# Decode attention with a gated FFN: one loop turn per head group on all engines, V in one load

## The chip, the core and the metric

The kernel runs on one core of one Trainium2 chip. The core has five engines that run their own instruction streams: TensorE (PE in the profile; its weight loads are PEld), VectorE (DVE), ScalarE (ACT), GpSimd (POOL) and SyncE (SP), which issues the transfers. They meet only at semaphores: an instruction may wait until a semaphore has reached a value, and may raise one when it is done. Data come from HBM over 16 DMA engines into SBUF (128 partitions); TensorE writes its results into PSUM. The metric is the device time of one execution in microseconds (us). Before the change it is 354.29 us, the median of three runs (353.94 to 354.31).

## The reference

One token passes through two branches, and a scalar gate mixes them. Branch A is attention over a cache: 32 query heads in 8 groups of 4, each group with its own K and V of 32768 rows of 128 numbers. Branch B is a SwiGLU feed-forward layer with 1792 hidden units.

```python
def _A_ref(x, k_cache, v_cache, wq, wo):          # x: (1, 1, 512)
    q = (x @ wq).reshape(B, Sq, 32, 128).transpose(0, 2, 1, 3)
    k = jnp.repeat(k_cache, 4, axis=1)             # k_cache: (1, 8, 32768, 128)
    v = jnp.repeat(v_cache, 4, axis=1)
    scores = jnp.einsum("bhqd,bhkd->bhqk", q, k) * (128 ** -0.5)
    p = softmax(scores, axis=-1)
    o = jnp.einsum("bhqk,bhkd->bhqd", p, v)
    return o.transpose(0, 2, 1, 3).reshape(B, Sq, 4096) @ wo

def _B_ref(x, w_gate, w_up, w_down):
    return (silu(x @ w_gate) * (x @ w_up)) @ w_down

x = A_x
g = sigmoid((x * gate_w).sum(-1, keepdims=True))
return g * _A_ref(x, ...) + (1 - g) * _B_ref(x, ...)
```

All arrays are bf16. K and V are 64 MiB each; with the weights the kernel reads 148.1 MB.

## The kernel before

**Pages.** SBUF holds five pages of 4 MiB (`page`, 128 partitions of 32 KiB). A page takes half of one group's K or V: block `b` (0 or 1) of 16384 rows, partition `p` holding 128 rows that follow each other. Pages 0 and 2 are for K, 1 and 3 for V; page 4 holds `wq` at first and `wo` at the end, and page 3 holds `w_gate` and `w_up` before V comes into it.

**Queue.** SP issues all transfers, in one order written out by hand: `wq`, `x`, `gate_w`, `w_gate`, `w_up`, then K and V pages, then `w_down` (`wd`) and `wo` in five pieces. From group 2 on, K block `b` of group `g` alternates with V block `b` of group `g-1`. A K page waits on `sem_fill` until its page has been transposed for the group before, a V page on `sem_v_free` until the matmuls on it are through. The very last V block goes into page 0, which K has left.

**Start.** `x` and `gate_w` are loaded as columns, 4 numbers per partition. POOL builds two identities, a permutation `pmat` and a selection `sel4` by `affine_select`, and sums the gate's product over the partitions (L263). PE makes q (L440, L457) and the hidden units of branch B (L470, L482), ACT the sigmoids, VectorE the rest.

**K block (`emit_k`).** A block has 8 units of 8 transposes. A unit transposes 16 rows of every partition (as fp32 pairs, L340) into one of two PSUM buffers `pst`; VectorE copies it to SBUF (`ktT`, L669); 16 matmuls of 8 columns make the scores (L352) in `ps_sc[b]`. PE runs two units ahead of the copies. VectorE then takes each partition's maximum (L674), for both blocks together L676.

**Softmax.** POOL takes the maximum over all partitions with `partition_all_reduce` (L268). ACT scales it to `nbias` (L553) and takes eight exponentials per group (L562, four heads by two blocks) that also sum.

**V block (`emit_v`).** 32 matmuls with 512 columns, in four strips of PE's columns (L399), add into `ps_o`. After both blocks ACT copies `ps_o` to `acc` (L574), PE reduces the strips by matmuls with `sel4` (`emit_reduce`, L378), and VectorE copies the result into `oT` (L660).

**Order of groups.** On PE the groups run in a hardware loop of 8 turns; a turn handles K block `b` of group `g`, then V block `b` of group `g-1`, for `b` = 0 and 1. Group 7's V comes in the end section. ACT, VectorE and POOL have their eight groups written out one after another. The exponentials of group `g` and the accumulator copy of group `g-1` so run on ACT while PE is at other work.

**End (`emit_end`).** V of group 7, the sum of exponentials for all 32 heads in one fp32 matmul (L501), the reciprocals, branch B's `wd` (L411, 14 matmuls), a scaled and transposed attention output (`oTs`, `O2a`, `O2`), and `wo` in strips of one row (L411) and, for its last eight pieces, in rows (L422). The end section stands in the code ahead of the start section; a loop of two turns and two branches select them.

Of the kernel before, what the change touches and what calls it, by code (L numbers as in the profile page):

```python
# [5 lines left out]
ACT = mybir.ActivationFunctionType  # L6
ALU = mybir.AluOpType
# [3 lines left out]
ReduceOp = bass.bass_isa.ReduceOp  # L11


def bass_gated_mix__gqa_block_cached__swiglu_ffn__decode_kernel(
# [27 lines left out]
    BLK = 128 * R  # L42
    NB = S // BLK
    assert S % BLK == 0 and NB == 2
# [22 lines left out]
    QT = H * DH // (NSTRIP * QN)  # L67
    assert QT == 2 and QN == 512 and F % (NSTRIP * FC) == 0 and FS <= 512
    assert RQ * HPG <= 32 and RQ * DH == 512

    PG_K = (0, 2)
    PG_V = (1, 3)
# [4 lines left out]
    with ExitStack() as es:  # L77
# [3 lines left out]
        sem_page = [S_(f"s_page{i}") for i in range(4)]  # L81
        sem_vl = S_("s_vl")
# [5 lines left out]
        sem_ld_wd = S_("s_ld_wd")  # L88
        sem_fill = S_("s_fill")
        sem_sc = S_("s_sc")  # L90
        sem_v_free = S_("s_v_free")
        sem_cp = S_("s_cp")
        sem_out = S_("s_out")
        sem_const = S_("s_const")
        sem_pool = S_("s_pool")
        sem_ident = S_("s_ident")
        sem_dchain = S_("s_dchain")
        sem_pz = S_("s_pz")
        sem_pe_t = S_("s_pe_t")
        sem_pe_part = S_("s_pe_part")  # L100
        sem_part = S_("s_part")
        sem_ps1 = S_("s_ps1")
        sem_pe_q = S_("s_pe_q")
        sem_pe_qp = S_("s_pe_qp")
        sem_pe_h = S_("s_pe_h")
        sem_pe_S = S_("s_pe_S")
        sem_pe_O2 = S_("s_pe_O2")
        sem_pe_sum = S_("s_pe_sum")
        sem_dve_prod = S_("s_dve_prod")
        sem_dve_gpart = S_("s_dve_gpart")  # L110
        sem_dve_qT = S_("s_dve_qT")
        sem_dve_t1 = S_("s_dve_t1")
        sem_dve_tr = S_("s_dve_tr")
        sem_dve_tm = S_("s_dve_tm")
        sem_dve_tT = S_("s_dve_tT")
        sem_pmax = S_("s_pmax")
        sem_dve_esum2 = S_("s_dve_esum2")
        sem_dve_oT1 = S_("s_dve_oT1")
        sem_dve_oT2 = S_("s_dve_oT2")
        sem_dve_O2 = S_("s_dve_O2")  # L120
        sem_dve_row = S_("s_dve_row")
        sem_act_g = S_("s_act_g")
        sem_act_sg = S_("s_act_sg")
        sem_nbias = S_("s_nbias")
        sem_ps0 = S_("s_ps0")
        sem_acc = S_("s_acc")
        sem_red = S_("s_red")
# [606 lines left out]
```

## Time and profile before

| what | value |
|---|---|
| median of three runs | 354.29 us |
| the profiled execution's own time | 354.33 us |
| its span, first to last instruction | 352.5 us |
| mean granted TensorE clock | 0.827 |
| PE matmul busy | 265.0 us (75%) |
| PE weight loads busy | 223.2 us (63%) |
| VectorE busy | 181.7 us (52%) |
| ScalarE busy | 33.1 us (9%) |
| GpSimd busy | 6.3 us (2%) |
| read from HBM | 148.11 MB, 420 GB/s over the span |
| instructions recorded | 8346 |

The page divides the span into 40 slices of 8.8 us and gives each engine's busy share in tenths. A matmul's record shows an operation in a pipeline, so a busy PE isn't a PE at its peak: eight transposes are 0.93 us apart from the next unit's scores although each record is longer. PE has a granted clock that changes between 0.50 and 1.00 within the run. In the timeline a line gives start, duration, engine, source line, operation, output and inputs, count, and in brackets the idle time before it and what ended that. In the list of waits a line gives the total wait in us, how often, and the longest. DMA work is best read from when its data land: the wait of the first instruction that reads them.

### The profile page before, as it was taken

The page shows a single profiled execution, that of the slowest core. Times are in us where ns is not written, and L with a number is a line of the kernel's source. Part 1 is how long each engine was busy: PE and PEld are TensorE (multiplying, and loading weights), DVE is VectorE, ACT ScalarE, POOL GpSimd, SP SyncE. Part 2 cuts the span into 40 slices and gives each one's busy share as a digit, 9 for nine tenths or more (in the row PEclk, how much of TensorE's full clock was granted, in tenths as well). Part 3 has the DMA queues.
Part 4 walks back from the last instruction along what each step waited for, and adds up shares of the span by engine and source line. Part 5 has one row for each costly group of instructions (what it writes and reads, how often), then busy time and mean ns, then how long its engine had stood idle before and what let it go on. Part 6 is the DMA issues. An engine that isn't in the chain of part 4 may idle for free.

```text
span 352.5 us, 8346 instructions
## 1 busy us (share of the span) xinstructions
PE 265.0 (75%) x3831; PEld 223.2 (63%) x3831; DVE 181.7 (52%) x192; ACT 33.1 (9%) x149; POOL 6.3 (2%) x26
## 2 busy tenths in 40 slices
PE   0343987997999969597797949694987959795385
PEld 0113986976887949395786839493967859493131
DVE  2044967653874938266563818283644838093000
ACT  1000000400040040002100040004000030004000
POOL 0200000000000000000000000000000000000000
PEclk9986989785998998969887978799885989599555
DMA  8999999999999999999999999999999999999993
GB/s 322 409 439 429 433 433 426 431 425 439 435 428 431 431 432 428 439 431 428 428 439 431 428 428 439 435 428 428 439 431 428 428 442 428 428 428 442 407 422 145
DMA packets 6208, 148.22 MB, mean 420 GB/s; under 512 B 952, under 2 KB 952, under 8 KB 1336
## 3 DMA queue, kind: packets, MB, share of 16 engines
q1 hardware_dynamic: 6200, 148.12, 98.1%
q8 instruction: 5, 0.08, 0.1%
q14 instruction: 3, 0.02, 0.0%
HBM read 148.11 MB, written 0.00 MB: 420 GB/s over the span
## 4 chain that ended last, share of the span: by engine, by line
DMA 65%; PE 30%; DVE 3%; SPq 1%; issue 1%
DMA page<-in_A_k_cache_dram 53%; PE pst L340 23%; DMA page<-in_A_wo_dram 12%; PE ps_sc L352 5%; DVE ktT L669 2%; PE ps_o L399 2%; PE pst L422 0%; PE ps_m L378 0%; SPq L304 0%; SPq L326 0%; SPq L275 0%; SPq L319 0%; SPq L300 0%; SPq L297 0%; SPq L296 0%
## 5 line engine op out<-in xcount | busy, mean ns | idle before, releaser
L669 DVE COPY ktT<-pst 128x2048 bf16<-128x2048 bf16 x128 | 156.0, 1224 | 108.5 <-PE pst L340 101.6
L340 PE MATMUL pst<-ident_f,page 128*128 128x128 f32 x1024 | 159.5, 314 | 40.9 <-DMA page<-in_A_k_cache_dram 39.4
L340 PEld LDWEIGHTS pst<-ident_f,page 128*128 128x128 f32 x1024 | 136.0, 163 | 51.5 <-DMA page<-in_A_k_cache_dram 46.9
L352 PE MATMUL ps_sc<-qcur,ktT 128*128 128x8 bf16 x2048 | 68.0, 166 | 8.6 <-DVE ktT L669 8.6
L352 PEld LDWEIGHTS ps_sc<-qcur,ktT 128*128 128x128 bf16 x2048 | 67.2, 97 | 11.4 <-DVE ktT L669 10.0
L399 PE MATMUL ps_o<-page,ET 128*16 128x512 bf16 x512 | 40.0, 468 | 6.4 <-DMA page<-in_A_v_cache_dram 6.4
L399 PEld LDWEIGHTS ps_o<-page,ET 128*16 128x16 bf16 x512 | 12.9, 101 | 22.9 <-issue 8.4
L553 ACT ACTIVATE nbias<-gmax 128x4 f32<-128x4 f32 x8 | 1.6, 205 | 267.0 <-POOL gmax L268 267.0
L562 ACT ACTIVATE ET<-ps_sc,nbias 128x128 bf16<-128x128 f32 x64 | 23.9, 555 | 0.6
L562 ACT ACTIVATION_READ_ACCUMULATOR ET<-ps_sc,nbias 128x1 f32 x64 | 18.2, 284 | 0.0
L674 DVE TENSOR_REDUCE pmaxf<-ps_sc 128x4 f32<-128x512 f32 x16 | 11.1, 692 | 10.4 <-PE ps_sc L352 10.4
L440 PE MATMUL pst<-page,xT 128*1 128x512 bf16 x32 | 3.6, 627 | 14.9 <-DMA xT<-in_A_x_dram 14.9
L378 PE MATMUL ps_m<-sel,acc 128*128 128x4 f32 x72 | 10.9, 275 | 4.1 <-ACT acc L574 4.1
L378 PEld LDWEIGHTS ps_m<-sel,acc 128*128 128x128 f32 x72 | 10.2, 220 | 5.5 <-ACT acc L574 5.5
L440 PEld LDWEIGHTS pst<-page,xT 128*1 128x1 bf16 x32 | 1.0, 115 | 16.6 <-issue 16.6
L268 POOL PARTITION_ALL_REDUCE gmax<-pmax x8 | 3.0, 374 | 291.8 <-DVE pmax L676 291.8
L660 DVE COPY oT<-ps_m 128x4 f32<-128x4 f32 x8 | 1.3, 157 | 13.2 <-PE ps_m L378 13.2
L574 ACT ACTIVATE acc<-ps_o 128x512 f32<-128x512 f32 x8 | 5.2, 652 | 14.8 <-PE ps_o L399 14.8
L603 DVE TENSOR_TENSOR prod_col<-xT,gwT 128x4 f32<-128x4 bf16 x1 | 0.2, 164 | 11.2 <-DMA gwT<-in_gate_w_dram 11.2
L470 PE MATMUL pst<-page,xT 128*1 128x448 bf16 x32 | 3.0, 553 | 1.7 <-DMA page<-in_B_w_up_dram 1.7
L411 PE MATMUL pst<-page,O 128*1 128x512 bf16 x24 | 2.9, 617 | 1.7 <-DMA page<-in_A_wo_dram 1.7
L482 PE MATMUL ps_m<-ones_bf,ktT 128*128 128x1 bf16 x14 | 1.0, 200 | 4.2 <-DVE ktT L649 4.2
(58 smaller groups left out, 31.9 us busy)
## 6 DMA issues: line engine op xcount, KB each, us to landing
page<-in_A_k_cache_dram SPq DMA_DIRECT2D x16, 4096.0 KB, 27.2
page<-in_A_v_cache_dram SPq DMA_DIRECT2D x16, 4096.0 KB, 31.7
page<-in_A_wq_dram SPq DMA_DIRECT2D x1, 4096.0 KB, 13.9
page<-in_A_wo_dram SPq DMA_DIRECT2D x1, 2048.0 KB, 39.6
page<-in_B_w_gate_dram SPq DMA_DIRECT2D x1, 1792.0 KB, 16.9
page<-in_B_w_up_dram SPq DMA_DIRECT2D x1, 1792.0 KB, 20.6
wd<-in_B_w_down_dram SPq DMA_DIRECT2D x1, 1792.0 KB, 35.1
page<-in_A_wo_dram SPq DMA_DIRECT2D x1, 1024.0 KB, 41.6
```

Of the source, the lines that this page charges most:

```text
L268: pool.partition_all_reduce(gmax[:, g, :], pmax[:, g, :], 128, ReduceOp.max).then_inc(sem_gmax, 1)
L340: ins = pe.transpose(pst[u % NST][:, k * 128 : (k + 1) * 128], kv[:, n * 128 : (n + 1) * 128], ident_f[:, :],)
L352: ins = pe.matmul(ps_sc[b][:, col : col + 2 * HPG], kt[:, k, e, :], qcur[:, e, :], start=(e == 0), stop=(e == 1),)
L378: ins = pe.matmul(ps_m[:, M_P0 : M_P0 + HPG], acc[:, q, :], sel4[:, q * HPG : (q + 1) * HPG], start=(q == 0), stop=(q == RQ - 1),)
L399: ins = pe.matmul(ps_o[32 * c : 32 * c + RQ * HPG, :], ET[:, n : n + RQ, :].rearrange("p n h -> p (n h)"), view[:, k * RQ : (k + 1) * RQ, ...
L411: return pe.matmul(ps_c[32 * c : 32 * c + 1, :], vec[:, j : j + 1], w[:, j, :], start=start, stop=stop, skip_group_check=True,)
L440: ins = pe.matmul(pst[0][32 * k : 32 * k + 1, t * QN : (t + 1) * QN], xT[:, c : c + 1], wq_v[:, c, n : n + QN], start=(c == 0), stop=(c == ...
L470: ins = pe.matmul(pst[1][32 * k : 32 * k + 1, w * 512 : w * 512 + FS], xT[:, c : c + 1], wgu[:, w, c, k * FS : (k + 1) * FS], start=(c == ...
L562: act.activation(ET[:, b * R : (b + 1) * R, h], sc[:, h, :], ACT.Exp, bias=nbias[:, g, h : h + 1], scale=SCALE, accum_out=esum[:, g, b, h ...
L574: act.activation(acc[:, :, :].rearrange("p q d -> p (q d)"), ps_o[:, :], ACT.Copy).then_inc(sem_acc, STEP)
L669: dve.tensor_copy(ktT[:, u % NKT, :], pst[u % NST][:, :].bitcast(BF16)).then_inc(sem_cp, 1)
L674: dve.tensor_reduce(pmaxf[:, f, :], sc, AX.X, ALU.max).then_inc(sem_pmax, 1)
```

## The change

All engines now run one hardware loop over the groups, and a turn does one group whole: K block 0, K block 1, the maximum, the exponentials, V, the accumulator copy, the reduction, the reciprocals. Semaphores rise by 16 a turn, so that each wait is the loop's register plus a constant.

- **Loads.** V of a group comes in one transfer of 8 MiB, 64 KiB for each partition, behind both K pages; for the last group in two. K is read as 32 KiB from every 64 KiB, so that a partition has the same 256 rows for K and V. Pages 0 and 1 are for K, 2 and 3 for V. The first V waits for the hidden units of branch B, which lie in page 3. POOL raises the second V semaphore for the groups with one load.
- **Maximum.** The POOL reduction becomes a PE transpose of the 128x4 maxima, a VectorE reduction to four numbers, their product with a 4x4 identity, and a PE matmul with ones that spreads them over the partitions. ACT reads the result from PSUM.
- **Sums.** The sum of exponentials becomes a matmul in every group, with reciprocal and gate on VectorE.
- **Start.** `x` and `gate_w` come as rows of one partition. PE turns `x` into columns (four matmuls) and makes the identity's argument: the row of 0 to 127 against its negative, by two matmuls with ones; VectorE compares with 0 and derives `ident`, `pmat` and `sel4`. The gate's sum is a VectorE reduction along the row and a matmul that spreads it. POOL has only two memsets, and neither library instruction is left.
- **End.** `emit_end` starts with branch B; V and reductions are all in the loop.

Core of the diff:

```diff
-    PG_K = (0, 2)
-    PG_V = (1, 3)
+    PG_K = (0, 1)
+    PG_V = 2
...
+                for g in range(G - 1):
+                    pool.wait_ge(sem_v[0], 16 * (g + 1))
+                    pool.sem_inc(sem_v[1], 16)
...
-                def load_v(g, b):
...
+                    src = A_k_cache[0, g, :, :].rearrange("(p b r) d -> p b r d", b=NB, r=R)
...
+                def load_v(g):
+                    if g:
+                        sp.wait_ge(sem_v_free, STEP * g)
+                    else:
                         sp.wait_ge(sem_pe_h, 1)
...
+                    if g < G - 1:
+                        sp.dma_start(
+                            vpage.rearrange("p b r d -> p (b r d)"),
+                            src.rearrange("p b r d -> p (b r d)"),
+                        ).then_inc(sem_v[0], 16)
...
+                sp.dma_start(x_row[0:1, :], A_x[0, :, :]).then_inc(sem_ld_x, 16)
+                sp.dma_start(gw_row[0:1, :], gate_w.unsqueeze(0)).then_inc(sem_ld_g, 16)
...
-                for b in range(NB):
-                    load_k(0, b)
-                load_v(0, 0)
-                load_k(1, 0)
-                load_v(0, 1)
-                load_k(1, 1)
-                for g in range(2, G):
+                for g in range(G):
                     for b in range(NB):
                         load_k(g, b)
-                        load_v(g - 1, b)
-                for b in range(NB):
-                    load_v(G - 1, b)
+                    load_v(g)
...
+                def emit_max(i):
+                    pe.wait_ge(sem_pm, i + STEP)
+                    pe.transpose(
+                        ps_m[0:HPG, M_A0 : M_A0 + 128], pmax[:, :], ident_f[:, :]
+                    ).then_inc(sem_t, STEP)
+                    pe.wait_ge(sem_dg, i + STEP)
+                    pe.matmul(
+                        ps_m[:, M_B0 : M_B0 + HPG],
+                        ones_f[0:HPG, :],
+                        diag[:, :],
+                        start=True,
+                        stop=True,
+                    ).then_inc(sem_b, STEP)
...
                 def emit_reduce(i):
-                    pe.wait_ge(sem_acc, i)
-                    pe.wait_ge(sem_rc, i)
+                    pe.wait_ge(sem_es, i + STEP)
+                    pe.matmul(
+                        ps_s,
+                        ones_f[:, :],
+                        esum2[:, :],
+                        start=True,
+                        stop=True,
+                    ).then_inc(sem_s, STEP)
+                    pe.wait_ge(sem_acc, i + STEP)
...
                     with pe.Fori(0, G * STEP, STEP) as i:
                         for b in range(NB):
                             emit_k(i, b)
-                            with pe.If(i > 0):
-                                emit_v(i, b)
+                        emit_max(i)
+                        emit_v(i)
+                        emit_reduce(i)
...
+                with act.Fori(0, G * STEP, STEP) as i:
+                    act.wait_ge(sem_b, i + STEP)
                     act.activation(
-                        nbias[:, g, :], gmax[:, g, :], ACT.Copy, scale=-SCALE
-                    ).then_inc(sem_nbias, 1)
...
+                        nbias[:, :], ps_m[:, M_B0 : M_B0 + HPG], ACT.Copy, scale=-SCALE
+                    ).then_inc(sem_nbias, STEP)
+                    act.wait_ge(sem_nbias, i + STEP)
...
+                    act.wait_ge(sem_v_free, i + STEP)
+                    act.activation(part, ps_o[:, :], ACT.Copy).then_inc(sem_acc, STEP)
...
+                with dve.Fori(0, G * STEP, STEP) as i:
                     for b in range(NB):
                         for u in range(UPP):
-                            dve.wait_ge(sem_fill, UPP * f + u + 1)
+                            dve.wait_ge(sem_fill, i + (UPP * b + u + 1))
...
+                    dve.wait_ge(sem_t, i + STEP)
+                    dve.tensor_reduce(
+                        gm[:, :], ps_m[0:HPG, M_A0 : M_A0 + 128], AX.X, ALU.max
+                    ).then_inc(sem_d, 1)
+                    dve.wait_ge(sem_d, i + 3)
+                    dve.tensor_scalar(
+                        diag[:, :], ident_f[0:HPG, 0:HPG], gm[:, 0:1], None, op0=ALU.mult
+                    ).then_inc(sem_dg, STEP)
+                    dve.wait_ge(sem_exp, i + STEP)
+                    dve.tensor_tensor(
+                        esum2[:, :], esum[:, 0, :], esum[:, 1, :], ALU.add
+                    ).then_inc(sem_es, STEP)
+                    dve.wait_ge(sem_s, i + STEP)
+                    dve.reciprocal(rS[:, :], ps_s).then_inc(sem_d, 1)
...
+                    dve.wait_ge(sem_red, i + STEP)
```

The semaphore on the exponentials that PE held ahead of a block's scores is gone, since V of the group stands between.

482 lines of the change are left out of this document (216 added, 266 removed).

## The prediction

> **What bounds the kernel now.** I read the page's slices and its chain first, then the waits, then the timeline of single groups.
>
> ```profile
> DMA  8999999999999999999999999999999999999993
> GB/s 322 409 439 429 433 433 426 431 425 439 435 428 431 431 432 428 439 431 428 428 439 431 428 428 439 435 428 428 439 431 428 428 442 428 428 428 442 407 422 145
> ...
> DMA 65%; PE 30%; DVE 3%; SPq 1%; issue 1%
> ```
>
> The queues are full from the first slice to the last. 148.1 MB at about 429 GB/s is 345 us of the 352.5 us span, so the kernel is bound by its bytes. The waits say how much room TensorE has:
>
> ```profile
> PE pst L340 <- DMA page<-in_A_k_cache_dram: 39.4, 13, 4.7
> PE ps_o L399 <- DMA page<-in_A_v_cache_dram: 6.4, 2, 6.1
> PE pst L440 <- DMA xT<-in_A_x_dram: 14.9, 1, 14.9
> ```
>
> TensorE waits 39.4 us for K and 6.4 us for V over eight groups, some 5.7 us a group. The last wait falls before the loop. So all that the change puts in line on TensorE must fit in those 5.7 us, or the bound moves.
>
> The rate of the loads: the first K page lands at 33.0, the last one, 28 pages later, at 306.36. That is 273.4/28 = 9.76 us for a 4 MiB page and **39.05 us for a group** of four pages.
>
> **What a group costs on TensorE.** In the timeline a K block (8 units of 8 transposes, VectorE copy, 16 score matmuls) comes in two prices, by the clock in which it begins:
>
> ```profile
> 81.95 5.38 PE L340 MATMUL pst<-ident_f,page 128*128 128x128 f32 x24 [2.32 <-DMA page<-in_A_k_cache_dram]
> ...
> 95.72 1.90 PE L399 MATMUL ps_o<-page,ET 128*16 128x512 bf16 x32
> 97.55 1.97 PE L340 MATMUL pst<-ident_f,page 128*128 128x128 f32 x16
> ...
> 109.35 1.03 PE L378 MATMUL ps_m<-sel,acc 128*128 128x4 f32 x8
> ```
>
> The block from 81.95 to 95.72 took 13.8 us: it followed a wait, and the granted clock was 0.50 for its first five microseconds. The one from 97.55 to 109.35 took 11.8 us at clock 1.00. Thirteen blocks after a wait lie between 12.7 and 13.8, about 13.2 on the mean. The clock falls when there is little work in a stretch of about 3.4 us (it changed at 36.4, 46.6, 50.0, 60.3, 67.1) and rises after a full stretch of work.
>
> **The change, part by part.** First the order of work. Before, K of one group stood beside V of the previous one, so maximum, exponentials and accumulator copy lay under matmuls. After, every engine does group g whole: K, K, maximum, exponentials, V, copy, reduction. What was hidden stands in line now. My sum for one group on TensorE:
>
> 1. First K block: 13.2 (it begins after a thin stretch, so at the low clock).
> 2. Second K block: 12.4. It follows the first with no gap. Group 0, the only such pair in the trace, took 13.2 for it, since the clock fell after the thin tail of the first block; the best block took 11.8. I take the middle.
> 3. From the last score to the first V matmul: 5.75, worked out here from these rows:
>
> ```profile
> 59.03 0.56 PE L352 MATMUL ps_sc<-qcur,ktT 128*128 128x8 bf16 x16 [0.54 <-DVE ktT L669]
> 59.63 0.69 DVE L674 TENSOR_REDUCE pmaxf<-ps_sc 128x4 f32<-128x512 f32 x1 [0.65 <-PE ps_sc L352]
> 60.35 0.16 DVE L676 TENSOR_TENSOR pmax<-pmaxf 128x4 f32<-128x4 f32 x1
> 60.43 0.17 DVE L680 COPY qcur<-qblk 128x16 bf16<-128x16 bf16 x1
> 60.62 0.39 POOL L268 PARTITION_ALL_REDUCE gmax<-pmax  x1 [34.79 <-DVE pmax L676]
> 61.04 0.20 ACT L553 ACTIVATE nbias<-gmax 128x4 f32<-128x4 f32 x1 [34.14 <-POOL gmax L268]
> 61.33 1.28 ACT L562 ACT_TABLE_LOAD   x1
> ```
>
> Scores end at 59.59, the pair maximum at 60.51: 0.92. In place of the POOL reduction (0.5 with its handover) come a transpose on PE (0.45; those of K take 0.27 to 0.48), a reduction of 4x128 (0.29: between 0.16 for a 128x4 one and 0.69 for 512), a product with the identity (0.15), a matmul of ones (0.5, two cold fp32 ones took 0.64), each with about 0.05 of handover: 1.6. Then `nbias` 0.2 and a gap of 0.1, four exponentials 1.6 (320.99 to 322.58). That makes 4.45.
>
> The changed kernel's instruction stream, as built, shows one thing that the diff does not: ACT has a table load at the top of its loop, ahead of the `nbias` activation, and this load carries the wait for the new matmul. Before it ran once in the whole loop (the row at 61.33, 1.28 us); now it is issued in all eight turns, inside the chain. I add 1.28 and keep 0 as the other end, since no row shows a reload of a set that is already in: 5.75.
>
> 4. V, 64 matmuls: 6.0. A block of 32 took 1.90 at clock 1.00 and 3.59 at 0.50. After 5.75 idle microseconds it begins low, and rises after 3.4 to 5.5 us: between 5.3 and 6.6. The exponentials of the second half (1.4 us) lie under the first half's matmuls. So does the load: V lands 29.3 us after the group's first K page, and V begins at 31.4.
> 5. Accumulator copy and handovers 0.75, reduction 1.03 (1.87 at the low clock), loop branch 0.15. The matmul of the exponent sums (two rows, 0.64) lies under the copy. Reciprocal and both VectorE products lie beside the reduction and the next block's first transposes (two units, 2 us); without that cover they'd cost some 0.6.
>
> Sum: 13.2 + 12.4 + 5.75 + 6.0 + 0.75 + 1.03 + 0.15 = **39.3 us, against 39.05 of the loads**. TensorE becomes the bound by a hair. K pages are requested 11 us and more before their transfer begins, V 13 us (V is freed 37.4 us into a group, its successor starts at 48.8), so the queues don't run dry: SP now holds V behind the previous group's last V matmul and K behind V, but both waits end early. Merging the V loads therefore costs nothing; a stall of more than 11 us would uncover it.
>
> On ACT, behind the wait in the table load, stand `nbias` and all exponentials, and V waits for them. On VectorE, the waits for exponentials, sums and reduction now stand ahead of the next group's copies; the last ends with the reduction, before PE has filled the first unit.
>
> Costed at nothing: register sums ahead of each VectorE wait (the sequencer does them while the 1.22 us copy runs; cover is thin, as a unit takes PE 1.31; I bound it by 0 and 0.08 per copy, 16 copies); identity built by matmul instead of POOL (both are done before `x` lands at 14.8); x as a row: its four matmuls and one copy add some 0.7 to a start that then waits 1.7 us for `w_up`.
>
> K at a pitch of 64 KiB and V in 64 KiB rows: no row has them. The nearest is the first `wo` load, 16 KiB pieces at twice that pitch: 2.1 MB in 4.9 us (wd done at 339.8, the strips released at 344.8), 428 GB/s, the common rate. I take no change and bound it by 2% of loss. The small pieces of x and gate_w (8 bytes each) go: the queues fell to 174 GB/s for 0.5 us at 12.0, so 0.3 us is won, to be had at most twice.
>
> 6. The end. Before, TensorE was early and waited for `wo`:
>
> ```profile
> 339.85 1.87 PE L378 MATMUL ps_m<-sel,acc 128*128 128x4 f32 x8 [0.75 <-ACT acc L574]
> 341.64 1.87 PE L411 MATMUL pst<-wd,tT 128*1 128x512 bf16 x14
> 344.81 1.87 PE L411 MATMUL pst<-page,O 128*1 128x512 bf16 x16 [1.15 <-DMA page<-in_A_wo_dram]
> ```
>
> From the end of the reduction (341.72) to the end of the span are 10.8 us; less 0.88, 0.54 and 0.21 of waiting for `wo`, 9.15 remain. After, all weights are there when TensorE comes, and the 9.15 follow in line. The jump out of the loop to the end section was hidden under a wait of 3.35 us before (ACT's copy, at 324.45) and is on the path now: 0.3, between 0 and 3.35. [...]
>
> Total: 32.7 + 8 × 39.3 + 9.15 + 0.3 = 356.5 of span, with the 1.8 between span and time (354.33 against 352.5; the profiled run is 0.04 above the median) **358.4 us**, 1.2% slower.
>
> **Rivals.**
> - *The table load costs nothing when the set is already in.* The group falls to 38.0, below the loads. Then the last group begins with its page at 306.1: 306.1 + 38.0 + 9.45 + 1.8 = 355.4. Still slower, as the end is in line. Chance 0.19.
> - *Nothing comes out late* (the other side): the clock stays high. Both K blocks at 11.8, no reload: V would be wanted at 28.1 and wait for its load, at 29.3; with 5 for V and 1.9 behind it the group ends at 36.2, and the last reduction at 342.3. That is 0.6 later than before, within the 1.63 of waiting for `wo`. The last `wo` piece then ends the kernel, 0.3 earlier for the x row: 354.0; with the 1 us lost in the first slice's ragged rates won too, 353.2. It decides below 36.7 per group. For it: seven V blocks directly after a K block ran at 1.90. Against: group 0's pair, and 5 us of idle ahead of each V. Chance 0.17, about half of it visibly faster.
> - *VectorE's register waits show.* 16 × 0.08 = 1.3 more, 40.6 per group: 32.7 + 324.8 + 9.45 + 1.8 = 368.8. Against: TensorE's own register waits in the same loop cost nothing visible. Chance 0.12.
> - *The new pitch slows the loads* by 2%: 39.8 per group, 362. Chance 0.05.
>
> [...] Chance of this rival 0.02.
>
> **Numbers.** The forecast, TensorE bound at 38.8 to 40.2 a group, has 0.45: 358.4, by itself 355.5 to 365.5. What a measurement here can tell from no change is about 0.2%, 0.7 us. Slower: 0.82, faster 0.09, same 0.09. The range, 354.1 to 366.5, reaches into the second rival and stops short of the third.
>
> **What would show it.** A table load in each of eight turns, directly after the matmul of ones; about 5.7 us between last score and first V; V blocks that begin at clock 0.5; waits of TensorE for K almost gone; first K blocks 39 to 39.5 apart; waits for `wo` gone at the end. The forecast is wrong if K waits remain at 2 us or more a group, or if VectorE's copies are more than 1.31 apart.

## The result and the profile after

| | before | after |
|---|---|---|
| median of six runs | 354.12 us (353.87 to 354.31) | 352.56 us (352.43 to 352.74) |
| ratio, 95% interval | 1 | 0.9957 [0.9944, 0.9969] |
| the profiled execution: time, span | 354.33, 352.5 us | 352.43, 350.6 us |
| mean granted TensorE clock | 0.827 | 0.867 |
| last packet of `wo` ended (packet records of the trace) | 349.25 us | 347.46 us |

The changed kernel is 0.44% faster; forecast was 358.4 us, 1.2% slower, and 352.56 lies below the range. The page of the changed kernel, its slices, its packets and its chain:

```profile
DMA  8999998999989999999999998999999999999994
GB/s 329 413 453 419 477 450 377 421 426 456 471 381 419 478 411 422 422 464 464 396 411 422 460 471 381 419 456 434 426 419 426 501 396 411 422 437 441 410 422 193
DMA packets 4914, 148.21 MB, mean 423 GB/s; under 512 B 554, under 2 KB 556, under 8 KB 940
...
DMA 61%; PE 30%; DVE 4%; ACT 2%; SPq 1%; issue 1%; ACTq 0%; DVEq 0%
```

The slices stay full up to the end, so the bytes are still the bound. The chain has ACT in it now (2%). The waits of TensorE (total, times, longest):

```profile
PE ps_o L332 <- ACT ET L530: 27.1, 8, 3.4
...
PE pst L279 <- DMA page<-in_A_k_cache_dram: 8.6, 6, 2.8
```

Waiting for K fell from 39.4 us to 8.6, and a wait for exponentials of 3.4 us in each of eight turns came in. No matmul waits for V in the list. So most of TensorE's room was spent, as forecast, but not all. V is not far away either: by the landing records of the trace, V of group 1 landed at 100.72 and its first matmul began at 102.23; in the tightest group the two are 0.6 us apart (255.92 and 256.54). The timeline of a whole turn, group 1, shows what it costs:

```profile
72.29 1.94 PE L279 MATMUL pst<-ident_f,page 128*128 128x128 f32 x16
...
84.06 1.94 PE L279 MATMUL pst<-ident_f,page 128*128 128x128 f32 x16
...
85.17 10.20 DVE L646 COPY ktT<-pst 128x2048 bf16<-128x2048 bf16 x8 [0.24 <-PE pst L279]
...
95.43 0.56 PE L291 MATMUL ps_sc<-qcur,ktT 128*128 128x8 bf16 x16 [0.54 <-DVE ktT L646]
...
96.03 0.69 DVE L651 TENSOR_REDUCE pmaxf<-ps_sc 128x4 f32<-128x512 f32 x1 [0.65 <-PE ps_sc L291]
96.82 0.16 DVE L653 TENSOR_TENSOR pmax<-pmaxf 128x4 f32<-128x4 f32 x1
...
97.13 0.37 PE L313 MATMUL ps_m<-ident_f,pmax 128*4 128x128 f32 x1 [1.14 <-DVE pmax L653]
97.54 0.28 DVE L661 TENSOR_REDUCE gm<-ps_m 4x1 f32<-4x128 f32 x1 [0.43 <-PE ps_m L313]
97.93 0.22 DVE L665 TENSOR_SCALAR diag<-ident_f,gm 4x4 f32<-4x4 f32 x1
...
98.29 0.55 PE L317 MATMUL ps_m<-diag,ones_f 4*128 4x4 f32 x2 [0.79 <-DVE diag L665]
98.92 1.28 ACT L523 ACT_TABLE_LOAD   x1 [27.60 <-PE ps_m L317]
100.22 0.17 ACT L523 ACTIVATE nbias<-ps_m 128x4 f32<-128x4 f32 x1
...
102.23 5.92 PE L332 MATMUL ps_o<-page,ET 128*16 128x512 bf16 x64 [3.38 <-ACT ET L530]
...
108.91 1.06 PE L353 MATMUL ps_m<-sel,acc 128*128 128x4 f32 x8 [0.45 <-ACT acc L539]
```

Read as steps: first K block 11.77, second 11.93 (84.06 to 95.99), last score to first V 6.24, V 5.92, copy and handover 0.76, reduction 1.06: 37.7 us for a group. Over all eight groups, from the first K page (32.69) to the end of the last reduction (342.14), less 5.8 us of waiting for K in between, it is 37.96. These are the K pages that TensorE waited for:

```profile
32.69 5.38 PE L279 MATMUL pst<-ident_f,page 128*128 128x128 f32 x24 [2.79 <-DMA page<-in_A_k_cache_dram]
110.47 4.41 PE L279 MATMUL pst<-ident_f,page 128*128 128x128 f32 x24 [0.50 <-DMA page<-in_A_k_cache_dram]
149.28 1.97 PE L279 MATMUL pst<-ident_f,page 128*128 128x128 f32 x16 [0.95 <-DMA page<-in_A_k_cache_dram]
188.08 4.50 PE L279 MATMUL pst<-ident_f,page 128*128 128x128 f32 x24 [2.10 <-DMA page<-in_A_k_cache_dram]
226.88 1.97 PE L279 MATMUL pst<-ident_f,page 128*128 128x128 f32 x16 [0.48 <-DMA page<-in_A_k_cache_dram]
```

A wait for a page that follows a page without pause marks when it landed: 38.80 us apart. The loads need 38.80 for a group, TensorE 37.7 to 38.0. The bound did not move. What the clock does in this turn and the next, in stretches: length, busy time of PE, PEld, DVE, ACT and POOL with the number of instructions, granted clock, DMA share, GB/s:

```profile
72.30:84.00 11.70, 10.72 (x192) 10.32 (x192) 9.87 (x9) 0.00 (x0) 0.00 (x0) 1.00 1.09 471
...
102.20:105.20 3.00, 2.97 (x32) 1.12 (x36) 0.16 (x1) 1.28 (x8) 0.00 (x0) 0.50 0.99 426
105.20:108.20 3.00, 3.00 (x41) 1.15 (x34) 0.00 (x0) 0.00 (x0) 0.00 (x0) 0.72 0.97 415
108.20:110.40 2.20, 1.32 (x10) 1.14 (x10) 0.57 (x3) 0.60 (x1) 0.00 (x0) 0.98 0.94 402
110.50:114.00 3.50, 3.50 (x18) 3.49 (x19) 1.23 (x1) 0.00 (x0) 0.00 (x0) 0.54 0.98 421
```

V begins at 0.50 after the chain, rises within its block, and the clock is 0.98 when it ends. The K block at 72.30, which had nothing to wait for, ran at 1.00 throughout; the one at 110.47, after a wait of 0.50 us, began at 0.54. A wait doesn't always bring the low clock: the blocks at 149.28, 226.88 and 265.69 came after waits of 0.95, 0.48 and 1.76 us and took 11.94 us each, at 1.00, while the second block of group 6 (277.49) stood right behind the first and took 13.13, with 3.4 us of it at 0.50.

The end, where TensorE still waits for `wo`:

```profile
341.08 1.06 PE L353 MATMUL ps_m<-sel,acc 128*128 128x4 f32 x8 [0.45 <-ACT acc L539]
342.06 1.03 PE L364 MATMUL ps_sc<-wd,tT 128*1 128x512 bf16 x14
...
345.39 0.60 PE L364 MATMUL ps_sc<-page,O 128*1 128x512 bf16 x8 [0.86 <-DMA page<-in_A_wo_dram]
346.66 0.39 PE L375 MATMUL ps_sc<-page,O 128*1 128x128 bf16 x16 [0.67 <-DMA page<-in_A_wo_dram]
...
347.96 0.28 PE L375 MATMUL ps_sc<-page,O 128*1 128x128 bf16 x8 [0.36 <-DMA page<-in_A_wo_dram]
```

### The profile page after: what moved, and what is told of

It is laid out like the page before. It is cut to its first block, busy times and chain, and to the rows that moved or that the text cites. A ratio compares the mean times of both kernels' runs of the same rounds, so it can differ in the third digit from the quotient of the medians.

```text
span 350.6 us, 8661 instructions
## 1 busy us (share of the span) xinstructions
PE 257.8 (74%) x3871; PEld 211.9 (60%) x3871; DVE 192.1 (55%) x242; ACT 43.0 (12%) x156; POOL 0.4 (0%) x6
## 4 chain that ended last, share of the span: by engine, by line
DMA 61%; PE 30%; DVE 4%; ACT 2%; SPq 1%; issue 1%; ACTq 0%; DVEq 0%
DMA page<-in_A_k_cache_dram 49%; PE pst L279 20%; DMA page<-in_A_wo_dram 12%; PE ps_sc L291 5%; DVE ktT L646 4%; PE ps_o L332 3%; ACT ET L530 1%; ACT L523 1%; SPq L265 0%; DVE pmaxf L651 0%; PE ps_m L317 0%; PE ps_m L353 0%; SPq L252 0%; PE ps_m L313 0%; SPq L244 0%
## 5 line engine op out<-in xcount | busy, mean ns | idle before, releaser
L646 DVE COPY ktT<-pst 128x2048 bf16<-128x2048 bf16 x128 | 155.5, 1224 | 30.2 <-PE pst L279 22.6
L279 PE MATMUL pst<-ident_f,page 128*128 128x128 f32 x1024 | 141.3, 287 | 14.0 <-DMA page<-in_A_k_cache_dram 8.6
L279 PEld LDWEIGHTS pst<-ident_f,page 128*128 128x128 f32 x1024 | 117.5, 147 | 17.6 <-DMA page<-in_A_k_cache_dram 9.1
L332 PE MATMUL ps_o<-page,ET 128*16 128x512 bf16 x512 | 44.8, 528 | 27.1 <-ACT ET L530 27.1
L332 PEld LDWEIGHTS ps_o<-page,ET 128*16 128x16 bf16 x512 | 16.4, 116 | 52.2 <-issue 41.2
L673 DVE RECIPROCAL rS<-ps_sc 128x4 f32<-128x4 f32 x8 | 1.5, 183 | 35.5 <-PE ps_sc L344 35.5
L353 PE MATMUL ps_m<-sel,acc 128*128 128x4 f32 x64 | 8.4, 255 | 3.6 <-ACT acc L539 3.6
L353 PEld LDWEIGHTS ps_m<-sel,acc 128*128 128x128 f32 x64 | 7.7, 191 | 4.3 <-ACT acc L539 4.3
L313 PE MATMUL ps_m<-ident_f,pmax 128*4 128x128 f32 x8 | 2.7, 333 | 9.1 <-DVE pmax L653 9.1
L317 PE MATMUL ps_m<-diag,ones_f 4*128 4x4 f32 x16 | 4.1, 326 | 6.3 <-DVE diag L665 6.3
L317 PEld LDWEIGHTS ps_m<-diag,ones_f 4*128 4x128 f32 x16 | 3.7, 282 | 8.3 <-issue 8.3
```

Of the source, the lines that this page charges most:

```text
L279: ins = pe.transpose(pst[u % NST][:, k * 128 : (k + 1) * 128], kv[:, n * 128 : (n + 1) * 128], ident_f[:, :],)
L313: pe.transpose(ps_m[0:HPG, M_A0 : M_A0 + 128], pmax[:, :], ident_f[:, :]).then_inc(sem_t, STEP)
L317: pe.matmul(ps_m[:, M_B0 : M_B0 + HPG], ones_f[0:HPG, :], diag[:, :], start=True, stop=True,).then_inc(sem_b, STEP)
L332: ins = pe.matmul(ps_o[32 * c : 32 * c + RQ * HPG, :], ET[:, n : n + RQ, :].rearrange("p n h -> p (n h)"), vpage[:, b, k * RQ : (k + 1) * ...
L353: ins = pe.matmul(ps_m[:, M_P0 : M_P0 + HPG], acc[:, q, :], sel4[:, q * HPG : (q + 1) * HPG], start=(q == 0), stop=(q == RQ - 1),)
L646: dve.tensor_copy(ktT[:, u % NKT, :], pst[u % NST][:, :].bitcast(BF16)).then_inc(sem_cp, 1)
```

## The experiments

Since the bytes set the pace, the question became what makes the same bytes take 1.5 us less. The trace also has every packet, a piece that one of the 16 queues moves at a time; their durations are used below.

**Pieces of 64 KiB, or the number of loads?** In the first kernel V comes in two loads in all groups. In the second V is one load, but in pieces of 32 KiB, since block `b` again has its own rows (K then also lies without a gap, as before).

```diff
# first kernel
-                for g in range(G - 1):
-                    pool.wait_ge(sem_v[0], 16 * (g + 1))
-                    pool.sem_inc(sem_v[1], 16)
...
-                    if g < G - 1:
+                    if g < 0:
# second kernel, for K and for V
-"(p b r) d -> p b r d", b=NB, r=R
+"(b p r) d -> p b r d", b=NB, r=R
```

> V comes in two loads of 4 MiB in every group, 32 KiB for each partition; all else as in the changed kernel. The changed kernel's K pages of one group land 38.83 us after those of the group before, against 39.05 before the change, and the first K page 0.33 earlier. Theory L (longer pieces: 64 KiB per partition cost less than twice 32 KiB): the spacing goes back to about 39.05, and the time rises by 7 x 0.2 = 1.4 to about 354.0. Rival N (fewer loads): the same 354.0. Rival P (the pitch of K rows) and rival O (the order of the loads): no change, 352.5, spacing 38.8.

> V stays one load per group, but K and V rows are taken block by block as before the change, so that a partition's V is two pieces of 32 KiB, 4 MiB apart, and K has the pitch of before. Theory L (length of a piece): 354.0, spacing 39.05. Rival N (number of loads): 352.5. Rival P (pitch): 354.0. Rival O (order): 352.5. With the run that splits V this separates all four: L high and high, N high and low, P low and high, O low and low.

Measured: 353.05 us (352.88 to 353.09) and 353.15 us (352.92 to 353.23), K pages 38.89 and 38.88 apart. A packet of 32 KiB takes 1216 ns in three cases of four, one of 64 KiB 2421: 11 ns less than two. 896 of them (seven loads) over 16 queues make 0.6 us, and K pages 0.09 us further apart over seven groups make the same. The times alone say less: these two ran on a chip on which the kernel before took 354.57 us, 0.45 more than beside the changed kernel, and their ratios to it (0.9959 and 0.9962) are that of the changed kernel. The nearest run with 64 KiB pieces on that chip is the one with columns below, whose packets take the same 1216 and 1224 ns: 352.66 us, 0.4 to 0.5 less. So the length of the piece counts, the number of loads does not, and the share is about a third of the gain.

**The pitch of K and V** alone, in the kernel before, beside that kernel as a control:

```diff
-                        which[0, g, b * BLK : (b + 1) * BLK, :].rearrange("(p r) d -> p r d", r=R),
+                        which[0, g, :, :].rearrange("(p b r) d -> p b r d", b=NB, r=R)[:, b, :, :],
```

> The kernel before, with the row mapping of the changed one alone: each page takes 32 KiB from every 64 KiB of K or V. Theory L (only the length of the pieces and the start count): same as before within 0.3. Rival P (the pitch itself makes the loads faster): 0.5 to 1.5 us below the kernel before, and the stall before the 29th page (20.41 between the last two K pages instead of 19.43) is gone.

> The kernel before once more, for a second profile. The first shows one load packet of 32 KiB at 293.8 that took 660 ns more than its 1215, and the last K page 0.98 late behind it. If that belongs to the kernel, it is there again at the same place; if it was chance, the last K page comes 19.43 behind the one before and the span is about 1 us shorter.

Measured: 354.39 us, ratio 1.0007 [0.9998, 1.0016]; the control 354.06. The pitch does nothing. The late single packets of the kernel before, near 132 and 294 us, are in both profiles again, so they belong to the program. So does the last K page, which comes 20.41 and 20.39 us after the K page ahead of it instead of 19.43 (landing records).

**The start.** One kernel uses GpSimd's library instructions once (one `affine_select`, one `partition_all_reduce`, on data that nothing reads), one loads `x` and `gate_w` as columns as well.

```diff
+                pool.affine_select(out=lib[:, :], in_=lib[:, :], ...)
+                pool.partition_all_reduce(lib2[:, :], lib[:, 0:1], 128, ReduceOp.add)   # first
...
+                sp.dma_start(xc[:, :], A_x[0, 0, :].rearrange("(p c) -> p c", c=KC))    # second
+                sp.dma_start(gc[:, :], gate_w.rearrange("(p c) -> p c", c=KC))
```

> POOL does one affine_select and one partition_all_reduce on tiles of its own at the start, as the only addition. If the GpSimd library had cost time before the change, the time rises by 0.3 us or more and the first K page lands later. My theory: nothing waits for POOL and the loads are not disturbed, 352.5, first K at 32.7.

> The two column loads of x and gate_w that the change removed are added again behind the row loads, into tiles that nobody reads. Theory: their small pieces hold the queues, the first K page lands 0.3 us later (33.0) and the time rises by 0.3 to 352.9. Rival: the earlier start has another source, the time stays at 352.5.

Measured: 352.59 us (352.18 to 353.05) and 352.66 us (352.53 to 352.82). Neither can be told from the 352.56 of the changed kernel. TensorE began on the first K page 0.25 us later with the columns (32.94 against 32.69), but that is no more than the scatter: it was 32.89 in the run with V in two loads, which has no columns, on the same chip. For the library a reserve holds, which the last experiments brought: its tiles shift the pages by 96 bytes, to a place where the changed kernel took 352.14 on another chip. It may cost up to 0.45, as much as the kernel before took longer on this chip.

**The chain in a turn.** Small activations were put ahead of `nbias`, between the matmul of ones and the exponentials, to use up TensorE's room: 6, 18 and 60 a turn.

```diff
                     act.wait_ge(sem_b, i + STEP)
+                    for k in range(6):        # 18, 60
+                        act.activation(dum[:, k, :], ps_m[:, M_B0 : M_B0 + HPG], ACT.Copy)
```

> Changed kernel with six more 128x4 activations on ACT in each turn, between the matmul of ones and nbias, their results read by nobody: 0.6 to 1.1 us more in the chain ahead of V. A turn of the changed kernel takes PE about 37.7 us without waits, and its K pages come every 38.8. Theory (the loads bound it, with 1.1 us of room on PE): the time stays within 0.4 of 352.6 while the waits of PE for K fall from 8.6 us towards 2. Rival (PE's chain bounds it already, the waits for K are remains): 8 x 0.6 to 1.1, 357 to 361.

> The same with eighteen activations: 1.8 to 3.3 us more per turn, 39.5 to 41.0. Theory: PE becomes the bound as the prediction had it; waits for K gone, time 32.7 + 8 x 39.5 to 41.0 + 8.2 + 1.8 = 359 to 371, and in the end section no wait for wo. If the time stays below 355, the room on PE is larger than I read.

> Sixty small activations ahead of nbias in each turn. Eighteen took 1.30 us and six 0.51, so sixty take 4.1; the table load then goes ahead of the wait and leaves the chain, 1.28 less: 2.8 us more than in the changed kernel. Theory (room of 1.1 us on PE, then PE is the bound): a turn takes 37.7 + 2.8 = 40.5, the last turn ends at 32.7 + 324, the time is 365 to 368 and PE no longer waits for K or wo. If the loads still bound it, 352.

With six, the premise failed. The timeline of ACT in that kernel:

```profile
98.02 0.51 ACT L525 ACTIVATE dum<-ps_m 128x4 f32<-128x4 f32 x6 [27.66 <-PE ps_m L318]
98.35 0.23 ACT L526 ACTIVATE nbias<-ps_m 128x4 f32<-128x4 f32 x1
```

The compiler put the table load ahead of the wait (at 69.07 for this turn), so that no load stands in the chain, and the wait of TensorE for exponentials fell from 3.38 to 2.44 us. Time: 352.14 us (352.01 to 352.23). It is thus the test of a shorter chain: 0.94 us less in each of eight turns, and at most 0.4 in the end; even that 0.4 has another cause (the place of the pages, below). In group 1 the shorter chain meets the load: V landed at 100.58, and its first matmul began at 100.62.

With 60, the chain is 2.65 us longer than in the changed kernel. The waits and two turns of that kernel:

```profile
PE ps_o L333 <- ACT ET L533: 48.3, 8, 6.0
```

```profile
73.51 1.94 PE L280 MATMUL pst<-ident_f,page 128*128 128x128 f32 x16
...
113.94 1.94 PE L280 MATMUL pst<-ident_f,page 128*128 128x128 f32 x16
```

TensorE waits for K once, ahead of the first group, and no longer for `wo`. A turn takes 40.43 us, and the time is 364.06 us (363.18 to 364.46), ratio 1.0274 [1.0258, 1.0289]. It is 1 us below the theory's range. The end section takes 6.6 us (356.07 to 362.67) without waits for `wo`, where it takes 8.46 in the changed kernel. Of 2.65 us a turn, 11.5/8 = 1.44 came through; the other 1.2 us was the room between TensorE's turn and the loads. This is the step at which the bound would have moved. The run is also the plain test of what a K block costs TensorE when it has nothing to wait for: all 15 blocks behind the first took 11.92 us at clock 1.00.

With 18 the chain is 0.14 us shorter than in the changed kernel (the table load is ahead of the wait here too), and the time was 351.03 us: 1.5 faster, which no theory had. It was run again, beside the changed kernel:

> The changed kernel once more, beside the next run on the same chip: 352.4 to 352.8, packets of 32 KiB 1217 to 1218 ns on the mean. If it comes out near 351.0, the 351.03 of the run with eighteen activations was chance of the placement.

> The run with eighteen activations once more. Before, it took 351.03 in four executions, 1.5 below the changed kernel, with every 32 KiB packet at 1212 to 1213 ns where all other runs have a quarter of the packets at about 1222. If that belongs to the kernel, 351.0 again; if it is where the arrays came to lie or what else the chip did, 352.0 to 352.7 with the mixed packets.

Measured: 352.46 us for the changed kernel, 350.88 (350.81 to 351.13) for the one with 18 activations, ratios to the kernel before 0.9955 [0.9941, 0.9968] and 0.9911 [0.9896, 0.9926]. The gain belongs to the program. In its trace 98% of the packets of 32 KiB take 1212 to 1214 ns, and the quarter at 1224 is gone.

**Streams written out.** The loops of VectorE and ACT in the changed kernel were written out, as before the change:

```diff
-                with act.Fori(0, G * STEP, STEP) as i:
+                for i in range(0, G * STEP, STEP):
...
-                with dve.Fori(0, G * STEP, STEP) as i:
+                for i in range(0, G * STEP, STEP):
```

> The changed kernel with the eight turns of VectorE and ScalarE written out again, with the same work and the same order; PE keeps its loop. (The table load then stands only in the first turn, and the chain is 1.28 us shorter in the others.) In the kernel before, two load packets late in the run, at 132 and 294, took 379 and 660 ns more than their like, in both of its profiles, and the last K page came 0.98 late behind the second; the changed kernel has none after 71 us. Theory F (long written-out streams have to be fetched piece by piece, and each fetch holds a load packet): late slow packets come back and the time rises by 0.3 to 1.0. Rival (they belong to the order of the loads): none after 80 us, and the time stays at 352.1 to 352.6. On the bound by the loads, the shorter chain gains nothing.

Measured: 352.55 us (352.50 to 352.79), ratio 0.9959 [0.9945, 0.9972]: no cost, beside 352.46 for the changed kernel on the same chip (run again, above). Late packets came back, 377 ns too long at 142 us and 659 ns at 229 us, the two sizes that the kernel before has (379 and 660), and one more at 76. The packet records show what stands ahead of each: a packet of 8 KiB of the kind `instruction`, at 142.28 and 229.16 here and at 132.12 and 293.94 in the kernel before, which takes 0.31 to 0.33 us; the late load packet starts when it ends. The queue lists of the kernel before, of the changed kernel and of this one have the line

```profile
q14 instruction: 3, 0.02, 0.0%
...
q14 instruction: 1, 0.01, 0.0%
...
q14 instruction: 3, 0.02, 0.0%
```

So theory F is right in its mechanism, fetches of written-out streams hold up load packets, and wrong in its price: they cost nothing that shows here, and the loops of VectorE and ACT are no part of the gain by the time. The run is also the cleanest test of a shorter chain, since the pages keep their place: seven of eight turns lack the table load, from the last score to V they take 4.65 to 5.36 us instead of 5.93 to 6.24, and the time stays.

**The place of the pages.** The activations need a tile, `dum`, and it lies ahead of `page`: with 18 of them the pages start at byte 38400 of each partition instead of 38112. (These bytes are added up from the sizes of the tiles in their order; the trace shows no addresses.) An unused tile alone does the same, in both kernels.

```diff
+        pad = T("pad", [128, 144], BF16)     # 288 bytes; 32 and 160; before: 320
         page = T("page", [128, NPG, PAGE], BF16)
```

> The changed kernel with an unused tile of 288 bytes per partition ahead of the tile `page` and nothing else. With 18 activations more (whose tile also took 288 bytes ahead of `page`) the kernel took 351.0 and 350.9 us instead of 352.5, and its transfers' packets of 32 KiB all took 1213 ns, where the changed kernel's take 1216 in three cases and 1224 in one. Theory P (place): what did it was the place of the pages in SBUF, byte 38400 of a partition, a multiple of 512, instead of 38112. Then this run gives 350.9 us (350.7 to 351.2) with packets of 1213 and 2418 ns. Rival T (time): the activations changed when transfers are requested or freed. Then it gives 352.5.

> As the last, with 32 bytes: the pages start at byte 38144, a multiple of 256 but not of 512. Theory P says only that the place counts. If a multiple of 256 (or of 64) is enough, 350.9 us; the changed kernel with 96 bytes more (a multiple of 64 alone) had packets of 1215 and 1222 and took 352.1. If 512 is needed, 352.1 to 352.5. Rival T: 352.5.

> The changed kernel with 160 bytes: the pages start at byte 38272, a multiple of 128 but not of 256. Theory P with the boundary at 128 or below: 350.9 us. With the boundary at 256 or 512: 352.1 to 352.5. Rival T: 352.5.

> The kernel before with an unused tile of 320 bytes per partition ahead of `page`: its pages start at byte 33280, a multiple of 512, instead of 32960. Theory P: packets of 1213 ns throughout; their mean was 1216.7, so the loads gain some 1.0 to 1.4 us and the kernel takes 352.7 to 353.2 us; the changed kernel, in the same place (the run with 288 bytes), then stays ahead by some 1.8 us, and the place is no part of what the change won. Rival T: 354.1, no change.

| kernel | first byte of the pages, rest to 256 | packet of 32 KiB, ns | time, us |
|---|---|---|---|
| after | 38112, 224 | 1216; a quarter 1221 to 1224 | 352.56 |
| after, six activations | 38208, 64 | 1215; a quarter 1220 to 1222 | 352.14 |
| after, 160 bytes | 38272, 128 | 1213 to 1216; half 1218 to 1221 | 352.11 (352.05 to 352.30) |
| after, 32 bytes | 38144, 0 | 1213, all | 351.03 (350.81 to 351.13) |
| after, 288 bytes | 38400, 0 | 1213, all | 351.00 (350.93 to 351.07) |
| before | 32960, 192 | 1215; a quarter 1220 to 1222 | 354.12 |
| before, 320 bytes | 33280, 0 | 1213, all | 352.65 (352.36 to 353.59) |

Theory P stands and T falls: no instruction was added, and 1.5 us are gone. A multiple of 256 is enough, 128 is not. The mean packet of 32 KiB falls from 1217.5 to 1213.1 ns (those above 1240 left out), and all packets of a queue together from 344.99 to 343.77 us: 1.2 of the 1.5 us. The K pages of the kernel with 288 bytes come 38.62 apart, and 77.40 for two groups:

```profile
109.92 4.38 PE L280 MATMUL pst<-ident_f,page 128*128 128x128 f32 x24 [0.69 <-DMA page<-in_A_k_cache_dram]
148.54 1.97 PE L280 MATMUL pst<-ident_f,page 128*128 128x128 f32 x16 [0.96 <-DMA page<-in_A_k_cache_dram]
225.94 4.38 PE L280 MATMUL pst<-ident_f,page 128*128 128x128 f32 x24 [0.88 <-DMA page<-in_A_k_cache_dram]
```

Both kernels had their pages at a bad place, and both gain the same from a good one (1.5 us). So the place is no part of what the change won: with both at a multiple of 256 the change is worth 352.65 - 351.03 = 1.6 us, as without (the kernel before with 320 bytes against itself: 0.9961 [0.9947, 0.9974]). Two of the five executions of that kernel took 353.5 us, so its median is less sure than the others.

**What the rest is.** Two last kernels, both at a good place: the kernel before with K, K, V, V in the queue, and the changed one with V in two loads.

```diff
-                load_v(0, 0)
-                load_k(1, 0)
-                load_v(0, 1)
-                load_k(1, 1)
-                for g in range(2, G):
+                for g in range(1, G):
                     for b in range(NB):
                         load_k(g, b)
-                        load_v(g - 1, b)
+                    for b in range(NB):
+                        load_v(g - 1, b)
```

> The kernel before with its pages at byte 33280 (320 unused bytes), and with both K pages of a group ahead of both V pages in the queue, as the changed kernel has them, where it alternated. It took 352.65 us with the alternating order; the changed kernel at such a place takes 351.0. Theory O: the order of the pages is a part of the 1.1 us that the piece length does not explain; then this run gives 351.5 to 352.0. Rival: the order has no part, 352.4 to 352.9, and the rest is left to the start and to how unevenly the 16 queues finish.

> The changed kernel with its pages at byte 38144 (32 unused bytes) and V in two loads of 32 KiB pieces. Theory L (length of the pieces): packets of 1213 ns twice against 2418 ns, 8 ns more for each of 1024 pairs over 16 engines: 0.5 us more than 351.03, so 351.4 to 351.7. If the 64 KiB pieces gain only where the pages lie badly: 351.0.

The second: 351.41 us (351.05 to 351.86), 0.4 more than with pieces of 64 KiB, and 0.5 more packet time per queue. Theory L holds at the good place too (with 896 pairs of packets, not 1024, as the last V comes in two loads in both kernels). The time of the first doesn't answer its question, since the loads ran dry: 359.75 us, ratio 1.0158 [1.0144, 1.0172]. Its slices:

```profile
DMA  8999498999999999999999999999999999999994
GB/s 328 406 437 445 207 394 317 463 410 443 436 414 465 410 432 444 418 454 421 425 451 414 447 432 414 462 414 436 440 418 458 418 429 444 418 451 429 413 424 193
```

In the fifth slice the queues run dry: K of group 1 waits for the pages of group 0, which TensorE has not yet read, and V, whose page is free, stands behind it. No byte moves from 41 to 45 us, and few from 55 to 57. From then on V comes late in each group. The wait of TensorE for it, from that kernel's list:

```profile
PE ps_o L397 <- DMA page<-in_A_v_cache_dram: 46.6, 8, 6.5
```

The trace answers the question all the same, since the queues are full from then on. The landing records give the distance of the K pages of one group from those of the group before, from group 3 to group 7:

| kernel, pages at a multiple of 256, pieces of 32 KiB | distance of K pages, us |
|---|---|
| before with 320 bytes, K and V alternating | 38.72, 38.72, 38.73, 38.72 |
| the same with K, K, V, V | 38.72, 38.73, 38.72, 38.73 |
| changed, 32 bytes, V in two loads | 38.73, 38.72, 38.73, 38.72 |

The order has no part in the pace of the loads. With V in pieces of 64 KiB (the changed kernel with 32 bytes) the mean is 38.69.

## Why the prediction was wrong

The cause in one sentence: **the sum for one group, 39.3 us, was 1.6 us too high, and 39.05 for the loads 0.25 too high; the true order is 37.7 under 38.80.** The bound stayed with the loads, and the gain at the edges could show. The forecast of 358.4 and the profiled 352.4 differ by 6.0 us: in seven turns that went at 38.83, the pace of the loads, instead of 39.3 (3.3 us), in the last turn, 37.65 instead of 39.3 (1.65), and in the end section, 8.46 instead of 9.45 (1.0).

1. *K blocks*, 13.2 and 12.4: **the step that failed.** They took 11.77 and 11.93 where TensorE did not wait, 2 us less in sum. The forecast let the first begin at the low clock after "a thin stretch"; in fact only the 0.76 us of the accumulator copy stand between V, reduction and K, and the clock is up again (0.98) before K begins. Where TensorE never waits for K, in the run with 60 activations, none of the 15 blocks behind the first paid the price of the low clock. In the changed kernel that price came behind waits for K (the block at 32.69: 13.84; at 110.47: 12.94), that is, mostly where there was time to lose, and once without (277.49: 13.13). The 13 blocks from which 13.2 was taken had all followed a wait. The only pair in the old trace stood at the start, and it was read as typical. The rule by which the forecast let the clock fall fits that trace only in part: each of its 18 falls came behind a stretch of 3.4 us in which matmuls were busy for at most 84%, but ten such stretches at the full clock brought none. In a second profile of the changed kernel the last group's first block, after a wait of 1.10 us, did take 13.92 us; the last reduction then ended 2.3 us later, TensorE found all of `wo` there, and that execution took 352.85 us, 0.4 more.
2. *Last score to first V*, 5.75: 6.24. The mechanism was right: the table load stands in all eight turns, 1.28 us, behind the matmul of ones. Transpose, reduction, product and spread took 1.86 from the end of `pmax` instead of 1.6, and the rest is handovers. With that the rival "the table load costs nothing" fell. Nothing more is lost behind the load in any of the eight turns (here it ends at 100.20 and `nbias` begins at 100.22).
3. *V, copy, reduction*: 5.92, 0.76 and 1.06 against 6.0, 0.75 and 1.03. Right for this turn, as is the low clock at V's begin; it rose within the block. Over the groups V took 5.0 to 5.9 us.
4. *Register waits of VectorE*: eight copies take 10.20 us, one each 1.28 us, as in the kernel before (seven in 8.88, one each 1.28) and below the 1.31 of a unit on TensorE. Nothing, as forecast; the rival of 368.8 fell.
5. *The loads*, 39.05: a mean over 28 pages, in which two landings came 0.35 and 0.98 us late. Undisturbed the old trace had 19.43 for two pages, 38.86. For the new pieces and the pitch a loss of up to 2% was allowed and no gain. The pitch did nothing, the pieces won 0.4 to 0.6 us by time and packets. A bound on one side only was the fault, since no row excluded a gain.
6. *The end*: 9.45 us in line behind the reduction. It took 8.46, and 1.89 of these are waits for `wo`: the strips ran at clock 1.00 (1.03 instead of 1.87 for 14 matmuls of `wd`). The jump out of the loop cost nothing: `wd` begins at 342.06, as the reduction ends.
7. *The start*, 32.7: 32.69.

What came true is the rival "nothing comes out late", given 0.17 and 354.0 or 353.2 us; 352.56 lies below both. Its reason, the clock that stays high, was right in the main. Its other condition, no reload, was not met, and its point of decision, 36.7 us a group, was too strict: it was worked out with an end at the low clock and slow loads. The two signs that the forecast named for being wrong did not show (K waits of 8.6/8 = 1.1 us a group, copies 1.28 us apart): they were set too wide to catch this error.

Where the 1.56 us come from can be read from the landing and packet records, where the two profiled executions are 1.90 us apart. The last packet of K and V ends at 335.00 us before and at 333.16 after, 1.84 earlier. Of this, 0.33 is there at the first K page (landed at 32.98 and 32.65); between two profiles of one kernel it moves by 0.15 and 0.25 (32.83 in the second of the kernel before, 32.90 in that of the changed one), so it is not shown to be a gain of the start. The pace, 38.86 against 38.80, gives 0.4: the 64 KiB pieces win 0.6, and the place of the changed kernel's pages costs 0.2 more than that of the kernel before. The largest part, 1.1, are pages that came late: 1.3 us before, 0.97 of it the last K page, against 0.2 after. That page came 0.95 to 0.98 us late in all four traces of the kernel before with its own order of loads (one with the other pitch, one with 320 bytes), and in each an 8 KiB instruction packet and a held-up load packet stand between 293 and 296 us. That the one caused the other is not shown: the changed kernel with written-out streams has the same packets, and none of its pages from group 2 on came more than 0.13 us late. Nor is it shown what the library (up to 0.45) or the columns of `x` cost.

The version that beats both kernels is the changed one with 32 bytes ahead of `page`: 351.03 us, ratio to the kernel before 0.9913 [0.9899, 0.9926].

## What to carry to other kernels

Where an engine is to take up the slack of a transfer-bound kernel, price its blocks in the state that they will have without waits: blocks that follow a wait may run at a low clock (here 12.9 to 14 us instead of 11.9, in some cases) and make the engine look busier than it will be. Take the pace of loads between undisturbed landings, not as a mean, and bound an unknown change of the transfers on both sides. And look at where tiles lie: starting the tile that all loads write at a multiple of 256 bytes gave 0.4%, about as much as the whole change.

## What the hardware showed

- A packet's time depends on the place in SBUF that it writes: 1213 ns for 32 KiB at a multiple of 256 bytes, on the mean 1217.5 in the changed kernel, 224 bytes past one; 2418 against some 2423 for 64 KiB.
- A table load repeated in every turn of a loop costs 1.28 us each time, and whether it stands ahead of a wait or behind it depends on the instructions next to it (six small activations moved it).
- Single load packets come late at like places in each profile of a program, right behind a packet of instructions. Behind those of 8 KiB near 132 and 294 us they were 0.38 and 0.66 us late with the pages at their old place, 0.25 and 0.53 with 320 bytes ahead of them. With written-out instruction streams there are three packets of 8 KiB, with loops one, and no effect on the time of the changed kernel could be seen.
- Queues that stood empty for some 6 us in sum between 40 and 57 us never made it up: the kernel ended 7.1 us later (359.75 against 352.65).
